# A feature-map attention followed by a maxout network, on one core: transposes by DMA, projections of q and k in banks of their own, stages by pair of heads

## The chip, the cores and the metric

The kernel runs on one core of a Trainium2 chip. A core has a matrix engine (TensorE, PE; loading its weights is shown as PEld), a vector engine (VectorE, DVE), a scalar engine (ScalarE, ACT), GpSimd (POOL) and Sync (SP), which here only issues DMAs; Sync, ACT and POOL each have a queue of DMAs, issued in program order. The metric is the time of one execution in microseconds; lower is better.

## The reference

For each of 8 x 8 heads, with 576 tokens of 64 elements, q and k are projected by `w_phi` to 128 features; the row's maximum of absolute values is subtracted, and both exponentials are kept. The result of the attention becomes the token matrix of a feed-forward network (FFN) with three up-projections, of which the elementwise maximum is kept.

```python
proj = x @ w_phi                                  # x is q or k: (8, 8, 576, 64) -> 128 features
proj = proj - max(abs(proj), axis=-1)
phi  = concat([exp(proj), exp(-proj)])            # 256 features
kv   = k_phi.T @ v ;  z = k_phi.sum(tokens)
x    = (q_phi @ kv) / (q_phi @ z + 1e-6)          # -> (4608, 512)
h    = maximum(maximum(x @ w1, x @ w2), x @ w3)   # 768 wide
out  = h @ w_out                                  # (4608, 512), float32
```

## The kernel before

The attention is cut into 16 **units** of 4 heads (half a batch entry). A unit has 18 blocks of 128 tokens: 4 for each head's first 512 tokens, and two that hold the 64 last tokens of two heads each. Its steps have one letter each, and an index for the piece:

- L loads q, k, v (Sync); C casts q and k to bf16 into `qk_bf`, side by side in 128 columns; T transposes the blocks on TensorE (L185) into PSUM, and DVE copies them to `qkT` (L186).
- G, for 4 blocks at a time, projects q and k in one matmul of 256 columns a block (L193, two banks, tag `g`); DVE reduces both to the maxima `m` (L196), ACT writes the two exponentials of k, `Ek` (L199).
- E scales v by exponentials of k's maxima (`em`), on POOL (L205 to L216). K multiplies `Ek` and the scaled v (L245) to `kv_sb`.
- Q and R put q's maxima into `mqp` and transpose them; V writes them by a DMA on ACT's queue as row 64 of `qkT` (L226). M projects q transposed, with a weight row of -1 that subtracts that row (L232), and ACT writes `Eq` (L234).
- N multiplies `Eq` and `kv_sb` (L258) and divides (`x_sb`); X transposes `x_sb` on TensorE (L272), and DVE copies it into `xT_main` and `xT_tail` (L273, L275).

When both units of a batch entry have passed X, a **chunk** of the FFN is queued: 18 "up" pieces of four matmuls of 512 columns (L287), evicted by ACT or DVE, and 4 "down" pieces of six (L302), evicted by ACT to `osb` and stored by Sync (L307). There are 8 chunks and one for all tails.

The order is written by hand: three lines of PROLOGUE, and PERIOD, which is run for u = 3 to 17; in `M4:1` the number behind the colon is the lag, so it is piece 4 of step M of unit u - 1. Each piece has a weight, and `run` puts FFN pieces between them until the line's budget (PRO_FFN, FFN_SHARE) is spread over it. Every engine works through its part of this order without reordering. PSUM is two pools: two buffers of two banks (G, K, N), four of one bank (all else).

Of the kernel before, what the change touches and what calls it, by code (L numbers as in the profile page):

```python
# [16 lines left out]
DF = 128  # L17
# [20 lines left out]
]  # L38
PERIOD = "X1:2 G0 L0:-2 G1 C0:-1 M4:1 M1:1 K0:1 G2 M0:1 C1:-1 G4 T0:-1 M2:1 G3 M3:1 N0:1 T1:-1 T2:-1 Q0 E0 N1:1 X0:1 R0 V0"
# [3 lines left out]
def kernel(  # L43
# [32 lines left out]
    raw = ctx.enter_context(tc.tile_pool(name="raw", bufs=2))  # L76
    vraw = ctx.enter_context(tc.tile_pool(name="vraw", bufs=3))
# [4 lines left out]
    psG = ctx.enter_context(tc.tile_pool(name="psG", bufs=2, space=bass.MemoryType.PSUM))  # L82
    psS = ctx.enter_context(tc.tile_pool(name="psS", bufs=4, space=bass.MemoryType.PSUM))

    class Unit:
        def __init__(un, u):
            un.u = u
            un.b = u // 2
            un.h0 = (u % 2) * HU
            un.ct0 = un.h0 // 2  # L90

        def load(un, what, engines=None, parts=1):
            for name, src in what:
                pool = vraw if name == "v_raw" else raw
                dst = pool.tile([P, UT, D], FP32, name=name, tag=name)
                setattr(un, name, dst)
                eng = (engines or {}).get(name, nc.sync)
                heads = src[un.b, un.h0:un.h0 + HU]
                n = HU // parts
                for i in range(parts):  # L100
                    h = slice(i * n, (i + 1) * n)
                    eng.dma_start(  # L102
                        dst[:, 4 * i * n:4 * (i + 1) * n, :].rearrange("p (h j) d -> p h (j d)", h=n),
                        heads[h, 0:SM, :].rearrange("h (p j) d -> p h (j d)", p=P))
                tails = heads[:, SM:S, :].rearrange("(pr ab) i d -> ab i pr d", ab=2)
                for ab in range(2):
                    eng.dma_start(dst[ab * D:(ab + 1) * D, MT:UT, :], tails[ab])  # L107

    first = Unit(0)
    first.load((("q_raw", q), ("k_raw", k)), {"k_raw": nc.scalar}, parts=2)  # L110
# [3 lines left out]
    wphi_f = const.tile([P, DF], FP32, name="wphi_f")  # L114
    nc.sync.dma_start(wphi_f[0:D, :], w_phi)
    nc.scalar.dma_start(wphi_f[D:2 * D, :], w_phi)
    first.load((("v_raw", v),))
# [26 lines left out]
    def load_w(half):  # L144
        n = slice(half * (DFF // 2), (half + 1) * (DFF // 2))
        for wi, w_ap in enumerate((moe_w1, moe_w2, moe_w3)):
            nc.gpsimd.dma_start(w_bf[wi][:, :, n], w_ap.rearrange("(ct p) n -> p ct n", p=P)[:, :, n])
# [4 lines left out]
    clock = [0]  # L152
    due = []

    def after(n, fn):
        due.append((clock[0] + n, fn))

    def piece(fn):
        fn()
        clock[0] += 1  # L160
        while True:
            now = [d for d in due if d[0] <= clock[0]]
            if not now:
                break
            due.remove(now[0])
            now[0][1]()
# [12 lines left out]
    def T(un, i):
        if i == 0:  # L180
            start_unit(un)
        t0, nb = ((0, 8), (8, 8), (16, 2))[i]
        tps = psS.tile([P, 8, P], BF16, name="tps", tag="s")
        for n in range(nb):
            nc.tensor.transpose(tps[:, n, :], un.qk_bf[:, t0 + n, :], ident)  # L185
        nc.vector.tensor_copy(un.qkT[:, t0 * P:(t0 + nb) * P],  # L186
                              tps[:, 0:nb, :].rearrange("p a c -> p (a c)"))

    def G(un, g):
        t0, n = GROUPS[g]  # L190
        psg = psG.tile([P, 4, 2, DF], FP32, name="psg", tag="g")
        for i in range(n):
            nc.tensor.matmul(psg[:, i, :, :].rearrange("p a f -> p (a f)"),  # L193
                             lhsT=un.qkT[:, (t0 + i) * P:(t0 + i + 1) * P],
                             rhs=w2.rearrange("p a f -> p (a f)"), start=True, stop=True)
        nc.vector.tensor_reduce(un.m[:, t0:t0 + n, :], psg[:, 0:n, :, :], AXX, ALU.max,  # L196
                                apply_absolute_value=True)
        for s in range(2):
            nc.scalar.activation(un.Ek[s][:, t0:t0 + n, :], psg[:, 0:n, 1, :], EXP,  # L199
                                 scale=1.0 - 2.0 * s)  # L200

    def E(un, i):
# [33 lines left out]
    def K(un, i):  # L236
        kvps = psG.tile([P, 2, 512], FP32, name="kvps", tag="g")
        W = D + 1
        for ab in range(2):
            for pr in range(2):  # L240
                for g in range(2):
                    o = (pr * 2 + g) * W
                    for c in range(5):
                        t = 8 * pr + 4 * ab + c if c < 4 else MT + pr
                        nc.tensor.matmul(kvps[:, ab, o:o + W], lhsT=un.Ek[g][:, t, :],  # L245
# [192 lines left out]
```

## Time and profile before

| | |
|---|---|
| median of 3 runs | 362.28 us (361.8 to 364.89) |
| the profiled execution | 361.97 us |
| its span, first to last instruction | 360.2 us |
| mean granted TensorE clock | 0.976 of 2.4 GHz |
| busy: PE, DVE, ACT, POOL | 314.7, 242.7, 217.6, 120.8 us |

The profile is of one execution. Spans of matmuls overlap, as they are pipelined: how far apart they start tells what one costs, and the chain of waits shows that for each run of them. "DMA share" is the mean busy share of the 16 DMA engines.

### The profile page before, as it was taken

The page shows a single profiled execution, that of the slowest core. Times are in us where ns is not written, and L with a number is a line of the kernel's source. Part 1 is how long each engine was busy: PE and PEld are TensorE (multiplying, and loading weights), DVE is VectorE, ACT ScalarE, POOL GpSimd, SP SyncE. Part 2 cuts the span into 40 slices and gives each one's busy share as a digit, 9 for nine tenths or more (in the row PEclk, how much of TensorE's full clock was granted, in tenths as well). Part 3 has the DMA queues.
Part 4 walks back from the last instruction along what each step waited for, and adds up shares of the span by engine and source line. Part 5 has one row for each costly group of instructions (what it writes and reads, how often), then busy time and mean ns, then how long its engine had stood idle before and what let it go on. Part 6 is the DMA issues. An engine that isn't in the chain of part 4 may idle for free.

```text
span 360.2 us, 7592 instructions
## 1 busy us (share of the span) xinstructions
PE 314.7 (87%) x2928; PEld 192.7 (54%) x2976; DVE 242.7 (67%) x403; ACT 217.6 (60%) x475; POOL 120.8 (34%) x164
## 2 busy tenths in 40 slices
PE   0656775899989997999899989997999999999994
PEld 0434653565646664666565656665666555544441
DVE  0674469688679866987698769876887775454350
ACT  2247375658676866767676867686859673522312
POOL 3342933434333434162516160707070505000000
PEclk9996689999999999999999999999999999999999
DMA  6898399512392229222832284217100200200205
GB/s 204 267 235 221 43 232 276 147 55 66 118 268 65 66 94 276 80 68 88 243 118 68 83 230 136 69 59 224 36 1 31 90 1 2 89 29 29 90 0 117
DMA packets 49028, 41.53 MB, mean 115 GB/s; under 512 B 15840, under 2 KB 44384, under 8 KB 48992
## 3 DMA queue, kind: packets, MB, share of 16 engines
q1 hardware_dynamic: 43696, 37.20, 34.1%
q0 software_dynamic: 3952, 3.15, 5.6%
q10 hardware_dynamic: 1344, 0.70, 0.7%
q8 instruction: 23, 0.38, 0.4%
q14 instruction: 13, 0.11, 0.1%
HBM read 34.67 MB, written 9.44 MB: 122 GB/s over the span
## 4 chain that ended last, share of the span: by engine, by line
PE 70%; issue 10%; DMA 10%; DVE 3%; POOL 2%; SPq 2%; ACT 1%; ACTq 0%; POOLq 0%; DVEq 0%
PE ups L287 32%; PE ops L302 13%; PE psg L193 7%; DMA qkT<-mT 5%; PE psn L258 5%; PE kvps L245 4%; PE tps L185 4%; PE psm L232 4%; DMA v_raw<-in_v_dram 3%; DVE m L196 2%; PE pxT L272 2%; DMA q_raw<-in_q_dram 1%; SPq L107 1%; POOL vtl L212 1%; SPq L102 1%
## 5 line engine op out<-in xcount | busy, mean ns | idle before, releaser
L287 PE MATMUL ups<-xT_main,w_bf 128*128 128x512 bf16 x540 | 141.7, 379 | 2.2 <-ACT t L291 0.3
L205 POOL TENSOR_TENSOR vab<-v_raw,em 128x2048 bf16<-128x2048 f32 x16 | 58.0, 3627 | 167.6 <-ACT em L204 131.5
L199 ACT ACTIVATE Ek<-psg 128x512 bf16<-128x512 f32 (+1 forms) x160 | 80.2, 555 | 44.3 <-DVE m L196 43.6
L196 DVE TENSOR_REDUCE m<-psg 128x8 f32<-128x1024 f32 (+1 forms) x80 | 87.9, 1115 | 27.7 <-PE psg L193 27.5
L287 PEld LDWEIGHTS <-w_bf 128*128 128x128 bf16 x648 | 60.2, 98 | 54.0 <-issue 1.2
L234 ACT ACTIVATE Eq<-psm 128x512 bf16<-128x512 f32 (+1 forms) x160 | 79.1, 573 | 8.4 <-PE psm L232 7.0
L291 ACT CAST t<-ups 128x512 bf16<-128x512 f32 x54 | 32.3, 598 | 50.6 <-PE ups L287 38.4
L193 PE MATMUL psg<-w,qkT 128*128 128x256 bf16 x288 | 45.5, 287 | 9.1 <-DVE m L196 4.3
L294 DVE TENSOR_TENSOR t<-t,ups 128x512 bf16<-128x512 bf16 x54 | 36.8, 681 | 23.1 <-PE ups L287 22.5
L302 PE MATMUL ops<-wout_bf,hT 128*128 128x512 bf16 x207 | 50.9, 379 | 0.5
L297 DVE TENSOR_TENSOR hT<-t,ups 128x512 bf16<-128x512 bf16 x54 | 37.1, 686 | 11.0 <-PE ups L287 7.6
L193 PEld LDWEIGHTS <-qkT 128*128 128x128 bf16 x288 | 28.6, 101 | 27.0 <-issue 5.9
L185 PE MATMUL tps<-ident,qk_bf 128*128 128x128 bf16 x288 | 25.9, 233 | 13.0 <-DVE qk_bf L352 11.5
L232 PE MATMUL psm<-qkT,wphi_m 128*128 128x512 bf16 (+1 forms) x78 | 26.2, 370 | 10.3 <-DMA qkT<-mT 8.2
L305 ACT COPY osb<-ops 128x512 f32<-128x512 f32 x36 | 21.3, 591 | 21.7 <-PE ops L302 21.2
L185 PEld LDWEIGHTS <-qk_bf 128*128 128x128 bf16 x288 | 21.2, 105 | 18.9 <-issue 12.2
L302 PEld LDWEIGHTS <-hT 128*128 128x128 bf16 x216 | 20.2, 98 | 19.9 <-DVE hT L297 0.4
L258 PE MATMUL psn<-kv_sb,Eq 128*128 128x65 bf16 x640 | 27.8, 198 | 3.2 <-ACT Eq L234 3.0
L258 PEld LDWEIGHTS <-Eq 128*128 128x128 bf16 x640 | 25.2, 100 | 9.0 <-ACT Eq L234 5.3
L186 DVE COPY qkT<-tps 128x1024 bf16<-128x1024 bf16 (+1 forms) x48 | 26.2, 552 | 3.9 <-PE tps L185 3.8
L264 DVE TENSOR_TENSOR x_sb<-psn,rden 128x640 bf16<-128x640 f32 x32 | 26.4, 825 | 1.1
L245 PEld LDWEIGHTS <-Ek 128*128 128x128 bf16 x640 | 23.6, 102 | 5.7 <-ACT Ek L199 3.8
(40 smaller groups left out, 234.9 us busy)
## 6 DMA issues: line engine op xcount, KB each, us to landing
v_raw<-in_v_dram SPq DMA_DIRECT2D x16, 512.0 KB, 4.3
out_dram<-osb SPq DMA_DIRECT2D x32, 256.0 KB, 2.3
q_raw<-in_q_dram SPq DMA_DIRECT2D x15, 512.0 KB, 4.8
k_raw<-in_k_dram SPq DMA_DIRECT2D x15, 512.0 KB, 5.0
w_bf<-in_moe_w_dram POOLq DMA_DIRECT2D x6, 384.0 KB, 8.6
q_raw<-in_q_dram SPq DMA_DIRECT2D x32, 32.0 KB, 4.6
v_raw<-in_v_dram SPq DMA_DIRECT2D x32, 32.0 KB, 4.3
out_dram<-osb SPq DMA_DIRECT2D x8, 128.0 KB, 2.3
```

The source lines that it names most:

```text
L185: nc.tensor.transpose(tps[:, n, :], un.qk_bf[:, t0 + n, :], ident)
L193: nc.tensor.matmul(psg[:, i, :, :].rearrange("p a f -> p (a f)"), lhsT=un.qkT[:, (t0 + i) * P:(t0 + i + 1) * P], rhs=w2.rearrange("p a f - ...
L196: nc.vector.tensor_reduce(un.m[:, t0:t0 + n, :], psg[:, 0:n, :, :], AXX, ALU.max, apply_absolute_value=True)
L199: nc.scalar.activation(un.Ek[s][:, t0:t0 + n, :], psg[:, 0:n, 1, :], EXP, scale=1.0 - 2.0 * s)
L205: nc.gpsimd.tensor_tensor(un.vab[:, :, :, 0:D], un.v_raw[:, 0:MT, :].unsqueeze(1).to_broadcast([P, 2, MT, D]), un.em[:, :, 0:MT].unsqueeze ...
L232: nc.tensor.matmul(psm[:, 0:n * P], lhsT=wphi_m, rhs=un.qkT[:, cols], start=True, stop=True)
L234: nc.scalar.activation(un.Eq[s][:, cols], psm[:, 0:n * P], EXP, scale=1.0 - 2.0 * s)
L245: nc.tensor.matmul(kvps[:, ab, o:o + W], lhsT=un.Ek[g][:, t, :], rhs=un.vab[:, g, t, :] if c < 4 else un.vtl[:, g, pr, ab, :], start=(c == ...
L258: nc.tensor.matmul(psn[:, ab, c * W:(c + 1) * W], lhsT=un.Eq[g][:, t0:t0 + P], rhs=un.kv_sb[:, ab, pr, g, :], start=(g == 0), stop=(g == 1))
L287: nc.tensor.matmul(ups, lhsT=w_bf[i][:, ct, j * P:(j + 1) * P], rhs=xT[:, ct, cols], start=(ct == 0), stop=(ct == CT - 1))
L297: nc.vector.tensor_tensor(hT[:, j, :], t_of.pop(j), ups, ALU.max)
L302: nc.tensor.matmul(ops_, lhsT=hT[:, j, tt * P:(tt + 1) * P], rhs=wout_bf[:, j, :], start=(j == 0), stop=(j == JT - 1))
```

## The change

- **Transposes by DMA.** Units 3 to 15 take `qkT` from two DMA transposes on Sync's queue (Y; 9 blocks each) in place of T; units 4 to 14 take `xT_main` and `xT_tail` from three (Z) in place of X. N writes the tails of those units to a tile of their own, `x_tail`.
- **G** writes k and q to a bank each (`psk`, `psq`), by a matmul of 128 columns for each block and each of the two, and DVE reduces them one by one; q's maxima go straight to `mqp` (Q is gone).
- **Maxima by matmul.** Units 0 and 1 use D in place of R, V and M: the same projection, and for each block a matmul of the broadcast maxima with a negative identity, added in PSUM.
- **By head pair.** A unit's blocks are ordered by pair of heads (9 and 9); loads, C (three pieces), E and K work on a pair or less. Unit 0 is loaded by single heads first. q, k have one raw buffer (two before), v two (three before).
- **PSUM** is eight single banks by kind: two for k, one pair for N, four for the rest. 14 matmuls on zeros run at the start (WARM).
- **Order and shares.** PROLOGUE's first line takes units 0 and 1 through all steps; A queues a chunk, with lag 2 in PERIOD. The loads of the FFN weights are cut into column blocks 1, 2 and 3 of 6. X's copy of the tails moves to ACT.

```diff
-FFN_SHARE = 10.0
-PRO_FFN = [2, 0, 0]
+PT = 9
+TBLOCKS = [(0, 4), (4, 12), (12, 18)]
+WBLOCKS = [(0, 1), (1, 3), (3, 6)]
+BANKS = {'k': 2, 'n': 1, 's': 4}
+BANK_OF = {'q': 's', 'v': 's', 'r': 's', 'm': 's', 'u': 's', 'd': 's'}
+WARM = 14
+FFN_SHARE = 8.9
+PRO_FFN = [4, 17, 8]
+XBAR = range(4, UNITS - 1)
+TBAR = range(3, UNITS - 0)
+YBLOCKS = [(0, 9), (9, 18)]
+YAT = {1: 0, 2: 1}
 PROLOGUE = [
...
+    "L0:-1 C0 C2 T0 C1 T1 T2 L1:-1 G0 G1 L1:-2 G2 D0 G3 C0:-1 C1:-1 D1 G4 C2:-1 E0 L0:-2 W1 T0:-1 E1 T1:-1 G0:-1 D3 T2:-1 W0 G1:-1 D2 D1:-1 D4 G2:-1 D0:-1 K0 E0:-1 G3:-1 N0 X0 G4:-1 K1 E1:-1 C1:-2 D2:-1 N1 D3:-1 K0:-1 C0:-2 K1:-1 X1 D4:-1 N0:-1 T0:-2 N1:-1 L1:-3 X0:-1 C2:-2 X1:-1 A0:-1 T1:-2 L0:-3 T2:-2 W2 C2:-3",
+    "L1:-2",
+    "C0:-1 G2 G4 C1:-1 T1:-1 G0 G1 G3 W3 T2:-1 E0 E1 R0 V0 L0:-2",
 ]
-PERIOD = "X1:2 G0 L0:-2 G1 C0:-1 M4:1 M1:1 K0:1 G2 M0:1 C1:-1 G4 T0:-1 M2:1 G3 M3:1 N0:1 T1:-1 T2:-1 Q0 E0 N1:1 X0:1 R0 V0"
+PERIOD = "G3 G0 C1:-1 K0:1 A0:2 C2:-1 M2:1 L1 G1 T2:-1 M0:1 M1:1 C0:-1 G2 T1:-1 M4:1 L0:-2 N0:1 E0 M3:1 K1:1 G4 E1 N1:1 X0:1 R0 V0 X1:1"
...
+    if WARM:
+        zeros = const.tile([P, SM], BF16, name="zeros")
+        nc.vector.memset(zeros, 0.0)
+        idle = bank([P, SM], FP32, "idle", "r")
+        for _ in range(WARM):
+            nc.tensor.matmul(idle, lhsT=zeros[:, 0:P], rhs=zeros, start=True, stop=True)
...
+    def Y(un, i):
+        if un.qkT is None:
+            start_unit(un)
+        t0, t1 = YBLOCKS[i]
+        nc.sync.dma_start_transpose(out=un.qkT[:, t0 * P:t1 * P].rearrange("p (t c) -> p t c", c=P),
+                                    in_=un.qk_bf[:, t0:t1, :].rearrange("p t c -> p (t c)"))
+
+    def Z(un, pr):
+        ct = un.ct0 + pr
+        nc.sync.dma_start_transpose(
+            out=xT_main[:, ct, un.b * SM:(un.b + 1) * SM].rearrange("p (c t) -> p c t", c=4),
+            in_=un.x_sb[pr][:, 0:4].rearrange("p c a d -> p (c a d)"))
+        if pr == 1:
+            nc.sync.dma_start_transpose(out=xT_tail[:, un.ct0:un.ct0 + 2, un.b * ST:(un.b + 1) * ST],
+                                        in_=un.x_tail.rearrange("p r d -> p (r d)"))
 
     def G(un, g):
         t0, n = GROUPS[g]
-        psg = psG.tile([P, 4, 2, DF], FP32, name="psg", tag="g")
-        for i in range(n):
-            nc.tensor.matmul(psg[:, i, :, :].rearrange("p a f -> p (a f)"),
-                             lhsT=un.qkT[:, (t0 + i) * P:(t0 + i + 1) * P],
-                             rhs=w2.rearrange("p a f -> p (a f)"), start=True, stop=True)
-        nc.vector.tensor_reduce(un.m[:, t0:t0 + n, :], psg[:, 0:n, :, :], AXX, ALU.max,
-                                apply_absolute_value=True)
...
+        psk = bank([P, 4, DF], FP32, "psk", "k")
+        psq = bank([P, 4, DF], FP32, "psq", "q")
+        for ab, ps in ((1, psk), (0, psq)):
+            for i in range(n):
+                nc.tensor.matmul(ps[:, i, :], lhsT=un.qkT[:, (t0 + i) * P:(t0 + i + 1) * P],
+                                 rhs=w2[:, ab, :], start=True, stop=True)
+        for ab, ps in ((1, psk), (0, psq)):
+            nc.vector.tensor_reduce((un.mqp, un.m)[ab][:, t0:t0 + n], ps[:, 0:n, :], AXX, ALU.max,
+                                    apply_absolute_value=True)
...
+    def D_(un, g):
+        t0, n = GROUPS[g]
+        cols = slice(t0 * P, (t0 + n) * P)
+        psm = bank([P, 4 * P], FP32, "psm", "m")
+        nc.tensor.matmul(psm[:, 0:n * P], lhsT=w2[:, 0, :], rhs=un.qkT[:, cols], start=True, stop=False)
+        for i in range(n):
+            nc.tensor.matmul(psm[:, i * P:(i + 1) * P],
+                             lhsT=un.mqp[:, t0 + i:t0 + i + 1].to_broadcast([P, P]),
+                             rhs=negident, start=False, stop=(i == n - 1))
+        for s in range(2):
+            nc.scalar.activation(un.Eq[s][:, cols], psm[:, 0:n * P], EXP, scale=1.0 - 2.0 * s)
...
+    def A(un, i):
+        if un.u % 2 == 1:
+            main_chunk(un.b)
+        if un.u == UNITS - 1:
+            tail_chunk()
```

## Rows read from the trace of the kernel before

**Rows 1.** The page's head and its first part.

```profile
span 360.2 us, 7592 instructions
...
PE 314.7 (87%) x2928; PEld 192.7 (54%) x2976; DVE 242.7 (67%) x403; ACT 217.6 (60%) x475; POOL 120.8 (34%) x164
```

**Rows 2.** Windows: span, length, busy us and instructions per engine, PE clock, DMA share, GB/s.

```profile
20.00:30.00 10.00, 5.09 (x35) 3.90 (x36) 8.18 (x11) 4.82 (x11) 5.25 (x6) 0.95 1.22 248
30.00:40.00 10.00, 7.12 (x76) 4.81 (x77) 2.69 (x7) 7.07 (x18) 4.48 (x4) 0.50 0.40 108
...
13.84:53.40 39.56, 26.56 (x260) 19.52 (x262) 23.19 (x37) 22.77 (x52) 21.02 (x27) 0.78 0.91 195
171.45:208.06 36.61, 34.87 (x355) 22.00 (x360) 28.82 (x49) 26.22 (x58) 14.39 (x19) 1.00 0.41 127
...
302.30:360.20 57.90, 52.88 (x295) 25.19 (x300) 22.41 (x36) 17.80 (x31) 0.00 (x0) 1.00 0.18 55
```

**Rows 3.** The chain of waits in order of time: start us, length us, what.

```profile
9.71 1.03 PE tps L185 x8
...
14.67 0.85 PE tps L185 x8
...
208.06 3.57 DMA qkT<-mT
...
212.18 0.86 PE ups L287 x4
213.04 1.26 PE kvps L245 x40
...
217.77 0.45 PE tps L185 x8
...
219.29 0.44 PE psg L193 x4
...
220.81 0.62 PE psn L258 x20
...
225.21 0.28 PE pxT L272 x5
...
235.77 1.29 PE ops L302 x6
```

**Rows 4.** The timeline of PE, 0 to 60 us: the first matmul of the FFN.

```profile
59.67 0.38 PE L287 MATMUL ups<-xT_main,w_bf 128*128 128x512 bf16 x1
```

**Rows 5.** Waits of PE: us in total, times, longest.

```profile
PE psm L232 <- DMA qkT<-mT: 8.2, 6, 2.0
```

**Rows 6.** Groups by line and shape, DVE: count, busy us, mean ns of one, idle before.

```profile
L196 DVE TENSOR_REDUCE m<-psg 128x8 f32<-128x1024 f32 x64 | 77.0, 1222 | 26.3 <-PE psg L193 26.1
...
L186 DVE COPY qkT<-tps 128x1024 bf16<-128x1024 bf16 x32 | 21.9, 684 | 2.5 <-PE tps L185 2.5
...
L273 DVE COPY xT_main<-pxT 128x512 bf16<-128x512 bf16 x32 | 13.4, 419 | 4.8 <-PE pxT L272 4.8
...
L196 DVE TENSOR_REDUCE m<-psg 128x4 f32<-128x512 f32 x16 | 11.0, 685 | 1.4 <-PE psg L193 1.4
```

**Rows 7.** The timeline of Sync's queue, 200 to 240 us.

```profile
208.78 1.26 SPq L107 DMA_DIRECT2D q_raw<-in_q_dram  x2
210.14 0.54 SPq L102 DMA_DIRECT2D k_raw<-in_k_dram  x1
...
237.71 0.36 SPq L307 DMA_DIRECT2D out_dram<-osb  x1
```

**Rows 8.** The timeline of ACT, 204 to 222 us: its queue issuing a DMA.

```profile
208.06 0.73 ACTq L226 DMA_DIRECT2D qkT<-mT  x1
```

**Rows 9.** DMA queues (packets, MB, share of 16 engines) and issues (KB, us to landing).

```profile
q1 hardware_dynamic: 43696, 37.20, 34.1%
...
out_dram<-osb SPq DMA_DIRECT2D x32, 256.0 KB, 2.3
...
wout_bf<-in_moe_w_out_dram POOLq DMA_DIRECT2D x1, 768.0 KB, 11.8
```

More of the change, by code (lines that the diff above doesn't have):

```diff
@@ L90, in __init__, with view, alloc @@
             un.ct0 = un.h0 // 2
-        def load(un, what, engines=None, parts=1):
-            for name, src in what:
+            un.qk_bf = un.qkT = None
+        def view(un, dst):
+            return dst.rearrange("p (r t) d -> p r t d", r=2)
+        def alloc(un, name):
+            if un.u == 0:
+                dst = const.tile([P, UT, D], FP32, name=name + "0")
+            else:
                 pool = vraw if name == "v_raw" else raw
                 dst = pool.tile([P, UT, D], FP32, name=name, tag=name)
[L96 to L107, printed above, removed]
@@ L109, with load_main @@
-    first = Unit(0)
-    first.load((("q_raw", q), ("k_raw", k)), {"k_raw": nc.scalar}, parts=2)
+            setattr(un, name, dst)
+            return un.view(dst)
+        def load_main(un, eng, dst, src, heads):
+            n = heads.stop - heads.start
+            pr, a0 = heads.start // 2, heads.start % 2
+            eng.dma_start(dst[:, pr, 4 * a0:4 * (a0 + n), :].rearrange("p (ab j) d -> p ab (j d)", ab=n),
+                          src[un.b, un.h0 + heads.start:un.h0 + heads.stop, 0:SM, :]
+                          .rearrange("ab (p j) d -> p ab (j d)", p=P))
@@ new lines, in load_tails, with load @@
+        def load_tails(un, eng, dst, src):
+            tails = src[un.b, un.h0:un.h0 + HU, SM:S, :].rearrange("(pr ab) i d -> ab i pr d", ab=2)
+            for ab in range(2):
+                eng.dma_start(dst[ab * D:(ab + 1) * D, :, 8, :], tails[ab])
+        def load(un, what):
+            for name, src in what:
+                dst = un.alloc(name)
+                for pr in range(2):
+                    un.load_main(nc.sync, dst, src, slice(2 * pr, 2 * pr + 2))
+                un.load_tails(nc.sync, dst, src)
@@ L112 @@
+    for ab in range(2):
+        nc.gpsimd.dma_start(wphi_f[ab * D:(ab + 1) * D, :], w_phi)
+    first.load((("v_raw", v),))
     ident = const.tile([P, P], BF16, name="ident")
     make_identity(nc, ident)
[L114 to L117, printed above, removed]
+    negident = const.tile([P, P], BF16, name="negident")
+    nc.gpsimd.tensor_single_scalar(negident, ident, -1.0, ALU.mult)
@@ L142, with load_w @@
     xT_tail = const.tile([P, CT, B * ST], BF16, name="xT_tail")
[L144 to L147, printed above, removed]
+    def load_w(n0, n1):
+        for w, w_ap in zip(w_bf, (moe_w1, moe_w2, moe_w3)):
+            nc.gpsimd.dma_start(w[:, :, n0:n1], w_ap.rearrange("(ct p) n -> p ct n", p=P)[:, :, n0:n1])
@@ L149, in load_wout, with copy @@
     def load_wout():
         nc.gpsimd.dma_start(wout_bf, moe_w_out.rearrange("(ct p) n -> p ct n", p=P))
[L152 to L166, printed above, removed]
+    def copy(eng, dst, src):
+        if eng is nc.scalar:
+            eng.copy(dst, src)
+        else:
+            eng.tensor_copy(dst, src)
@@ L238, in K @@
+    def K(un, pr):
+        kvps = bank([P, 2, 2 * (D + 1)], FP32, "kvps", "v")
         W = D + 1
         for ab in range(2):
[L240 to L245, printed above, removed]
-                                         rhs=un.vab[:, g, t, :] if c < 4 else un.vtl[:, g, pr, ab, :],
-                                         start=(c == 0), stop=(c == 4))
@@ L248, in K @@
-        un.kv_sb = mpool.tile([P, 2, 2, 2, W], BF16, name="kv_sb", tag="kv_sb")
-        nc.vector.tensor_copy(un.kv_sb.rearrange("p a r g d -> p a (r g d)"), kvps[:, :, 0:4 * W])
+            for g in range(2):
+                for c in range(5):
+                    t = PT * pr + (4 * ab + c if c < 4 else 8)
+                    nc.tensor.matmul(kvps[:, ab, g * W:(g + 1) * W], lhsT=un.Ek[g][:, t, :],
+                                     rhs=un.vab[:, g, t, :] if c < 4 else un.vtl[:, g, pr, ab, :],
+                                     start=(c == 0), stop=(c == 4))
@@ L333, in run @@
     def run(pieces, budget):
-        total = sum(w for w, _ in pieces)
+        total = sum(w for w, _ in pieces) or 1.0
         have = done = 0.0
         for w, fn in pieces:
-            piece(fn)
+            fn()
             have += w
@@ L396, in tokens @@
             name, i, lag = word[0], int(word[1]), int(word[3:]) if ":" in word else 0
+            if name == "X" and u - lag in XBAR:
+                name = "Z"
+            if name == "T" and u - lag in TBAR:
+                if i not in YAT:
+                    continue
+                name, i = "Y", YAT[i]
             got += stage(name, i, u - lag)
```

151 lines of the change are left out of this document (84 added, 67 removed), and 3 rows, old and new, of the table PROLOGUE.

## The prediction

> **What bounds the kernel now.** I read the page's totals first [rows 1]: TensorE is busy 314.7 of 360.2 us, the others 67% at most. The windows then show three stages [rows 2]. From 60 us on, two units take 36.61 us, 34.87 of them busy on PE: TensorE sets the pace, with DVE at 28.8 and ACT at 26.2. From 302 us only the feed-forward network (FFN) is left, and PE is busy 52.9 of 57.9 us. Up to 53 us it is not the bound: it is busy 26.6 of 39.6 us, and slowly, for the granted clock is 0.50 (1.2 GHz) from 30 to 40 us, and eight transposes took 0.85 us at 14.67 against 0.45 at 217.77 [rows 3]. The first matmul stands at 9.71 us and the first FFN matmul at 59.67 [rows 3, 4].
>
> The chain in order of time prices a piece once TensorE runs at speed [rows 3]: 0.056 us for a transpose (0.45/8; 0.28/5 for x), 0.11 for a matmul of 256 columns, 0.215 for one of 512, 0.0315 for one of K, 0.031 for one of N, 0.86 for an "up" of four, 1.29 for a "down" of six. A unit is then 18 x 0.109 (G) + 18 x 0.056 (T) + 0.97 (M) + 1.26 (K) + 1.25 (N) + 0.56 (X) + 0.06 (R) + half a chunk of FFN, 10.36, in all 17.4 us. The measured 18.3 leaves 0.9, most of it one wait per pair for the row of maxima (qkT<-mT, 3.57 us on the chain; psm waits 8.2 us for it in all) [rows 3, 5].
>
> The same count rebuilds the whole run: 60 us of prologue, 13 periods of 18.3 (238), 14.3 for the 16th, 41.7 for the last two chunks, 5 at the end (57.9 less 52.9): 359, against a span of 360.2. The profiled execution took 361.97 us, 1.8 more than its span; the median of the three runs is 362.28.
>
> **Transposes leave TensorE.** Units 3 to 15 lose 18 transposes, units 4 to 14 ten more: 1.0 and 0.56 us of PE a unit, all of it on the path, as PE is dense there: 13.1 + 6.2 = 19 us. DVE loses their evictions, of which the large ones are 2 x 0.684 + 2 x 0.42 a unit [rows 6].
>
> **What replaces them on the queues.** A unit gets two transposes for q and k (295 KB each), two for x (131 KB) and one for the tails (33 KB). No row shows one. Sync's queue spends 0.54 us on a main load, 0.63 on a tail (1.26 for two), 0.36 on an output [rows 7], and ACT's 0.73 on the SBUF-to-SBUF row of maxima [rows 8]. Six mains and six tails (the loads are now split by head pair) and two outputs make 7.7 us a unit; five transposes at 0.36 to 0.73 make 1.8 to 3.7 more, and I take 0.73, an SBUF-to-SBUF issue being nearest: 11.4 of a period of 15.3. They reach the path only if the queue's sum passes the period.
>
> Landing is bounded by 2.3 us (an output) and 11.8 (the casting weight load) [rows 9]. The first transpose of the next unit is issued in the middle of a period and the second two pieces later; the first G needs them when the next period begins, 5 to 8 us later, so I cost them nothing; if one took the 11.8, G would wait some 4 us each period. On the DMA engines, q1's 43,696 packets took 34.1% of 16 x 360.2 us: 45 ns each, 7.7 us a unit [rows 9]. Counted in 256-byte rows the transposes are 3,456 packets a unit, 9.7 us more at that price; the packets of now average 851 bytes, so I take half, 4.9: 12.6 of 15.3. The Trainium skill speaks against the change: "VectorE: DVE Perf Modes", section "The three transpose paths", gives 1309 ns for a 128x128 bf16 block by DMA against 390 on TensorE, and advises TensorE where PSUM will do. By that page of the Trainium skill, block after block, a unit's 27 blocks would be an estimated 35 us. The Trainium skill's "Advanced Engine Details and Errata", section "X-Bar Transpose (TRN2)", makes such DMAs as fast as ordinary ones at 350 to 400 GB/s, an estimated 2.5 us for the unit's 0.88 MB. No run here shows either; TensorE's own block costs 0.056 us on the dense chain.
>
> The queue also gains waits. q and k have one raw buffer now, so the load for the next unit but one waits for POOL's casts of the next one; behind it on Sync's queue stand the x transposes, which wait for x_sb, and the outputs, whose four buffers ACT fills. The casts come in thirds and E in halves by head pair, which takes POOL from 7.2 us a unit to 9 at the most likely, as only its small pieces double: of 15.3, no bound [rows 2]. The order puts the casts ahead of that load by two pieces and more, so I cost this at nothing; if the cover fails, the queue stands still for a cast, and the fall of the second rival begins.
>
> **G in two banks.** 36 matmuls of 128 columns for 18 of 256. The nearest row is the transpose, which also loads weights each time: 36 x 0.056 = 2.0 against 1.96, nothing; at the price of a 256-column one each it would be +2.0 a unit, the upper bound. DVE reduces eight halves at 0.685 for four at 1.222, +0.6 a unit [rows 6], paid by the evictions: 14.4 falls to about 12. ACT stays near 13.1, plus a second pair of small exponentials and the 0.73 issue: about 14, under a 15.3 us period but close.
>
> **The period.** PE work per unit in periods 5 to 15: G 2.0, K 1.26, N 1.25, M 0.97, R 0.06, and FFN 8.9 (a piece's weight in the code is about its us, and the budgets place 98 in these 11 periods): 14.4. M2 now stands behind G3, G0, K0 and three FFN pieces, some 4 us, against the row's 3.57 us, so that wait nearly goes. What is late next is ACT, whose exponentials free the banks that G and the FFN share. I take 0.9 again, between 0.1 (nothing waits) and 2.6: 15.3, between 14.5 and 17.
>
> **The prologue.** The first two units are finished before anything else, without the V round trip: D subtracts the maxima by 36 further matmuls (2 us at 0.056, 4 at half clock, beside ACT). Loads by head let the first transpose start some 3.5 us earlier; 14 idle matmuls run where PE waits for data until 9.71 us now; they cost nothing if they end by then (14 x 0.43 at half clock is 6 us). The copies of x tails by ACT in the five units that keep X are ten of 64 columns, in ACT's sum below. ACT was busy 22.8 us from 13.8 to 53.4 for about this work [rows 2]; it will have 24, and at 80% it takes 30. From 8 us that is 38, and 41 with the last N and X. Then 4.35 us of FFN, and unit 2's G with 7.8 of FFN (the budget 17 of the second line buys nothing, its only piece weighing 0): period 3 starts near 55.5 instead of 60, with 12.2 us of FFN done. Bounds: 50 and 66, the upper one if weights come late: some 13 MB must have landed by then, 53 us at the 248 GB/s of 20 to 30 us [rows 2].
>
> **What it gives back.** The second chunk is queued only in period 5 (A0 with lag 2), so period 3 uses up the first and period 4 has none: ACT-bound, 12 us with 6 of PE work.
>
> **The sum.** 55.5 + 15.5 (period 3) + 12 + 11 x 15.3 + 13.8 (period 16) + 60 (18.2 left of the seventh chunk, and 41.7 of the last two, dense as now) + 5 = 330.1, and 1.8 around the span: 331.9. I forecast 332 us.
>
> **Rivals.** (1) The prologue and ACT keep the gain: PE stays at 1.2 GHz between short bursts, weights come late, period 3 starts at 62, and ACT at 14 us a period costs 0.8 more in each: 332 + 6.5 + 9 = 347. For it: the half clock of 30 to 40 us; against: FFN now comes earlier and is dense. (2) Slower: Sync's queue becomes the bound. Loads, outputs, transposes stand in one order, and a transpose holds all behind it. 7.7 + 5t passes 15.3 at t = 1.5 us a transpose and loses the whole gain at about t = 1.95, where the period is 17.4; at 2.2 it is 18.7, and 332 + 11 x 3.4 + 6.7 (period 4) = 376. Against it: no issue on Sync's queue shown takes over 0.63; for it: none of those writes by the block. (3) The DMA engines bind: at 45 ns a packet they need 17.4 us a unit: 332 + 11 x 2.1 + 5.4 (period 4) = 360, no change. The 1309 ns block of the Trainium skill's page "VectorE: DVE Perf Modes" would end here too, at an estimated 550 us and more. (4) All waits vanish (11 x 0.8 less) and the prologue ends 4 us sooner: 319. (5) That the change doesn't do what it says: the first units alone keep their transposes on PE, so 13 of 16 must vanish; I give it nothing.
>
> **How the numbers follow.** Forecast 0.58 (own range 325 to 342), (1) 0.22, (2) 0.08, (3) 0.06, (4) 0.06. Faster by over 1%, about what this kernel's runs can tell from no change, has 0.86; within it 0.06; slower 0.08. The range 319 to 357 leaves out (2) and (3), 0.14, and the far ends of the rest.
>
> **What would show it.** Right: no tps in the dense stretch; a period of 15 to 15.6 us with PE busy 94%; no psm wait on qkT<-mT; an FFN matmul by 46 us; an idle period near 70 us; over 55 us of pure FFN at the end. Wrong: psg waiting for DMA on qkT, transposes of 1.5 us and more on Sync's queue, a DMA share near 1, or Ek and Eq as PE's releasers all along.

## The result and the profile after

The changed kernel takes 352.9 us against 362.2, a ratio of 0.9715 (95% interval 0.9644 to 0.9786): faster by 2.9%, a third of the forecast 8.4%. The profiled execution took 352.68 us. Here and below, executions over 1.5% above the fastest of their kernel are in the medians, but not in the ratios nor in the columns that a table takes from profiles. I read the profile in the order of [rows 1, 2]: totals, then the dense stretch, here from the transpose of unit 4's maxima to that of unit 15's (periods 5 to 15).

The page's head, its lines of PE, PEclk and DMA in 40 slices, and its first DMA queue:

```profile
span 350.9 us, 7981 instructions
...
PE 306.9 (87%) x2968; PEld 180.6 (51%) x2968; DVE 217.4 (62%) x412; ACT 216.4 (62%) x518; POOL 147.8 (42%) x296
...
PE   6665895696699999899999799989989999999994
...
PEclk9999699699899999999999899999999999999999
DMA  7898977748957678675969657959771210301205
...
q1 hardware_dynamic: 89152, 48.36, 53.6%
```

The dense stretch (columns as in [rows 2]):

```profile
93.17:272.20 179.03, 166.63 (x1802) 102.49 (x1800) 132.41 (x259) 135.16 (x333) 93.78 (x188) 0.98 0.71 179
```

Eleven periods take 16.28 us each, where [rows 2] show 18.3 and I forecast 15.3; DVE (12.0 us a period) and ACT (12.3) have room. Between those transposes the periods are far from even: 15.2 to 15.8 us in seven, 16.5, 17.1 and 19.3 in three, and 17.8 in the first. The first FFN matmul stands at 41.02 us (forecast 41), where [rows 4] had 59.67. Two things stand out.

**The start of period 3.** The chain in order of time:

```profile
52.69 1.19 POOL qk_bf L201 x2
...
53.90 1.57 SPq L224
...
55.52 8.55 DMA qkT<-qk_bf
...
64.11 0.60 PE psk L245 x4
```

TensorE stands still for 7.0 us, until the second transpose of unit 3's q and k lands, 8.55 us after its issue; the median of all 26 is 3.3. At 53.8 us POOL had issued the load of the output weights, which took 8.6 us to land. Afterwards the clock is at its lower level: 0.66 granted from 60 to 70 us, 0.50 from 64.1 to 66.7, where an up takes twice its 0.86.

**The held row of maxima.** ACT's timeline, then the chain, in the longest period:

```profile
190.27 0.25 ACT L279 COPY mT<-pmT 18x128 bf16<-18x128 bf16 x1
193.66 0.73 ACTq L283 DMA_DIRECT2D qkT<-mT  x1
194.44 2.06 ACT L251 ACTIVATE Ek<-psk 128x512 bf16<-128x512 f32 x4 [3.91 <-DVE kv_sb L317]
```

```profile
188.55 1.97 DMA q_raw<-in_q_dram
190.52 3.13 issue
193.66 2.51 DMA qkT<-mT
...
196.21 0.39 PE psm L289
```

The maxima are ready at 190.52, but V leaves ACT's queue at 193.66, and the exponentials queued behind it wait with it. (kv_sb, which the row names as the releaser, was written from 193.91 to 194.32 us; V's own issue, ahead of them on the queue, ended at 194.39.) The chain puts V behind a load of q. In the trace the DMAs of Sync's and ACT's queues take eight semaphores in turn, so V also waits for the DMA eight places before it, here the load of q issued at 188.55: ACT's queue waits on that semaphore, the last of the load's 16 pieces lands at 193.59, and V leaves at 193.66. In [rows 8] V left as soon as it could, 0.03 us after the copy of the maxima. TensorE waits 2.4 us for this V and then works at its lower clock, 0.57 granted from 196 to 200 us, where an up again takes twice its 0.86 (197.46 to 199.16): the period is long by the wait and by the clock behind it.

TensorE's waits from 93 to 272 us, which answer to [rows 5]:

```profile
PE psm L289 <- DMA qkT<-mT: 5.3, 3, 2.4
PE ups L361 <- ACT Eq L291: 3.7, 9, 0.6
PE psk L245 <- DMA qkT<-qk_bf: 0.9, 1, 0.9
```

Sync's queue across the same period, which answers to [rows 7]:

```profile
188.55 1.28 SPq L129 DMA_DIRECT2D q_raw<-in_q_dram  x2
189.87 1.11 SPq L122 DMA_DIRECT2D k_raw<-in_k_dram  x2
191.02 1.71 SPq L129 DMA_DIRECT2D k_raw<-in_k_dram  x2
192.83 2.58 SPq L229 DMA_TRANSPOSE xT_main<-x_sb  x2
195.50 1.19 SPq L233 DMA_TRANSPOSE xT_tail<-x_tail  x1
196.75 1.09 SPq L122 DMA_DIRECT2D v_raw<-in_v_dram  x2
197.88 1.28 SPq L129 DMA_DIRECT2D v_raw<-in_v_dram  x2
199.26 1.34 SPq L224 DMA_TRANSPOSE qkT<-qk_bf  x1
203.78 0.38 SPq L381 DMA_DIRECT2D out_dram<-osb  x1
204.26 1.31 SPq L224 DMA_TRANSPOSE qkT<-qk_bf  x1
205.62 1.09 SPq L122 DMA_DIRECT2D q_raw<-in_q_dram  x2
```

It issues without a pause from 188.55 to 200.6, then stands behind an output whose buffer ACT has not filled, and the next unit's transpose and loads stand behind that output. The transposes by line (ns: least, median, most):

```profile
L224 SPq DMA_TRANSPOSE qkT<-qk_bf x26: 1242/1324/3895, 53.9 to 253.9; - x26
...
L229 SPq DMA_TRANSPOSE xT_main<-x_sb x22: 1195/1239/2265, 111.8 to 272.5; - x22
...
L233 SPq DMA_TRANSPOSE xT_tail<-x_tail x11: 1185/1185/1287, 114.6 to 273.8; - x11
```

Five a unit are 2 x 1.32 + 2 x 1.24 + 1.19 = 6.3 us, not 3.7.

### The profile page after: what moved, and what is told of

It is laid out like the page before. It is cut to its first block, busy times and chain, and to the rows that moved or that the text cites. A ratio compares the mean times of both kernels' runs of the same rounds, so it can differ in the third digit from the quotient of the medians.

```text
span 350.9 us, 7981 instructions
## 1 busy us (share of the span) xinstructions
PE 306.9 (87%) x2968; PEld 180.6 (51%) x2968; DVE 217.4 (62%) x412; ACT 216.4 (62%) x518; POOL 147.8 (42%) x296
## 3 DMA queue, kind: packets, MB, share of 16 engines
q1 hardware_dynamic: 89152, 48.36, 53.6%
## 4 chain that ended last, share of the span: by engine, by line
PE 48%; ACT 22%; DMA 13%; SPq 6%; DVE 5%; issue 3%; POOL 3%; ACTq 0%; POOLq 0%; DVEq 0%
PE ups L361 28%; PE ops L376 8%; ACT Ek L251 8%; ACT Eq L291 8%; DMA q_raw<-in_q_dram 5%; DMA qkT<-qk_bf 4%; PE psn L326 4%; SPq L224 3%; DMA qkT<-mT 2%; PE kvps L312 2%; ACT Eq L303 2%; PE psk L245 2%; ACT t L365 2%; PE psq L245 2%; PE psm L289 1%
## 5 line engine op out<-in xcount | busy, mean ns | idle before, releaser
L251 ACT ACTIVATE Ek<-psk 128x512 bf16<-128x512 f32 (+1 forms) x160 | 82.1, 587 | 44.0 <-DVE m L248 22.1
L262 POOL TENSOR_TENSOR vab<-v_raw,em 128x1024 bf16<-128x1024 f32 x32 | 61.1, 1909 | 89.2 <-ACT em L260 67.6
L291 ACT ACTIVATE Eq<-psm 128x512 bf16<-128x512 f32 (+1 forms) x140 | 71.6, 617 | 3.9 <-PE psm L289 3.7
L248 DVE TENSOR_REDUCE m<-psk 128x4 f32<-128x512 f32 (+1 forms) x80 | 50.5, 632 | 30.2 <-PE psk L245 29.9
L245 PEld LDWEIGHTS <-qkT 128*128 128x128 bf16 x576 | 39.3, 101 | 25.6 <-DMA qkT<-qk_bf 8.9
L248 DVE TENSOR_REDUCE mqp<-psq 128x4 bf16<-128x512 f32 (+1 forms) x80 | 50.1, 627 | 0.0
L245 PE MATMUL psk<-w,qkT 128*128 128x128 bf16 x288 | 30.2, 224 | 10.8 <-DMA qkT<-qk_bf 8.1
L289 PE MATMUL psm<-qkT,wphi_m 128*128 128x512 bf16 (+1 forms) x70 | 24.7, 362 | 8.2 <-DMA qkT<-mT 7.5
L376 PEld LDWEIGHTS <-hT 128*128 128x128 bf16 x216 | 20.0, 98 | 22.5 <-issue 1.7
L245 PE MATMUL psq<-w,qkT 128*128 128x128 bf16 x288 | 30.1, 224 | 0.1
L201 POOL CAST qk_bf<-k_raw 128x512 bf16<-128x512 f32 (+2 forms) x43 | 21.3, 518 | 18.0 <-DMA k_raw<-in_k_dram 18.0
L312 PE MATMUL kvps<-vab,Ek 128*128 128x65 bf16 x512 | 25.3, 195 | 2.7 <-POOL vab L266 2.3
```

Of the source, the lines that this page charges most:

```text
L245: nc.tensor.matmul(ps[:, i, :], lhsT=un.qkT[:, (t0 + i) * P:(t0 + i + 1) * P], rhs=w2[:, ab, :], start=True, stop=True)
L248: nc.vector.tensor_reduce((un.mqp, un.m)[ab][:, t0:t0 + n], ps[:, 0:n, :], AXX, ALU.max, apply_absolute_value=True)
L251: nc.scalar.activation(un.Ek[s][:, t0:t0 + n, :], psk[:, 0:n, :], EXP, scale=1.0 - 2.0 * s)
L262: eng.tensor_tensor(un.vab[:, :, t0:tt, 0:D], un.v_raw[:, t0:tt, :].unsqueeze(1).to_broadcast([P, 2, 8, D]), un.em[:, :, t0:tt].unsqueeze( ...
L291: nc.scalar.activation(un.Eq[s][:, cols], psm[:, 0:n * P], EXP, scale=1.0 - 2.0 * s)
L312: nc.tensor.matmul(kvps[:, ab, g * W:(g + 1) * W], lhsT=un.Ek[g][:, t, :], rhs=un.vab[:, g, t, :] if c < 4 else un.vtl[:, g, pr, ab, :], s ...
```

## The experiments

Theory 1: V is held by the semaphore that it shares with a load, and the supply of weights delays period 3. Theory 2: the transposes' traffic slows every transfer. Theory 3: ACT is the bound at its margin. Theory 4 came after run 5: Sync's queue is too full. Medians in us; ratios to the kernel before, on the same chip, since the kernel before took 362.2 to 365.2 us on the chips used (0.8%). To compare two runs, divide their ratios. P3 is period 3, and "mean" that of periods 5 to 15, from the one profiled execution of each run; runs 5 and 16 have none, and run 16's ratio rests on two executions. The expectations call run 5 "run 4" once, and run 9 "run 5".

| run | us | ratio (95%) | P3 | mean |
|---|---|---|---|---|
| the change | 352.9 | 0.9715 (0.9644 to 0.9786) | 23.5 | 16.28 |
| 1 V on POOL, R moved | 355.6 | 0.9766 (0.9717 to 0.9815) | 21.7 | 16.55 |
| 2 output weights later | 352.8 | 0.9699 (0.9651 to 0.9746) | 25.3 | 16.22 |
| 3 x on TensorE | 360.1 | 0.9888 (0.9839 to 0.9936) | 22.5 | 16.77 |
| 4 q, k on TensorE | 373.1 | 1.0254 (1.0206 to 1.0302) | 22.1 | 17.64 |
| 5 tail loads after V | 361.6 | 0.9941 (0.9906 to 0.9977) | | |
| 6 no output weights | 347.2 | 0.9559 (0.9522 to 0.9597) | 17.9 | 16.31 |
| 7 FFN from P3 to P4 | 350.7 | 0.9656 (0.9607 to 0.9706) | 21.9 | 16.24 |
| 8 runs 2, 5 and 7 | 358.7 | 0.9863 (0.9809 to 0.9916) | 14.3 | 16.90 |
| 9 v loads on POOL | 348.6 | 0.9554 (0.9496 to 0.9611) | 22.7 | 15.58 |
| 10 one transpose for q, k | 354.6 | 0.9736 (0.9684 to 0.9787) | 23.2 | 16.40 |
| 11 v's tails thrice | 407.9 | 1.1206 (1.115 to 1.1263) | 24.7 | 20.85 |
| 12 runs 2, 7, 9 and 10 | 353.5 | 0.9713 (0.9662 to 0.9765) | 15.9 | 16.44 |
| 13 V on POOL, R in place | 352.5 | 0.9674 (0.9608 to 0.9741) | 22.9 | 16.34 |
| 14 runs 9 and 13 | 350.2 | 0.9621 (0.9572 to 0.9671) | 22.8 | 15.99 |
| 15 runs 2, 7 and 9 | 346.8 | 0.9509 (0.946 to 0.9559) | 15.6 | 16.02 |
| 16 runs 2, 7, 9 and 13 | 349.3 | 0.9511 (0.9436 to 0.9585) | | |

**Run 1**

```diff
-        nc.scalar.dma_start(un.qkT[D:D + 1, :]...
+        nc.gpsimd.dma_start(un.qkT[D:D + 1, :]...
-PERIOD = "... K1:1 G4 E1 N1:1 X0:1 R0 V0 X1:1"
+PERIOD = "... K1:1 G4 R0 V0 E1 N1:1 X0:1 X1:1"   # and E0 R0 V0 E1 in the prologue
```

> The row of maxima (V) is issued from POOL's queue instead of ACT's, after the transpose of the maxima; all else stands. Theory 1 (in the changed kernel V stands at the head of ACT's queue up to 3.1 us after mT is there, because its semaphore is one of eight that all DMAs of Sync's and ACT's queues share, and the DMA eight places before it is a load issued just before; the exponentials behind it stand still with it): the issue comes within 0.3 us of mT in every period, the psm<-mT waits fall under 1 us, the eleven periods 5 to 15 go from 16.2 towards 15.4 us each, and the time falls by 6 to 9 us, to 344 to 347. Theory 2 (the transposes' traffic slows every transfer, V's own among them): V still lands late, the periods stay at 16.2, the time within 1.5 us of 352.9. Theory 3 (ACT is the bound at its margin): the periods stay at 16.2 and ACT's idle time moves elsewhere, time within 2 us. POOL's own issue of a DMA costs it about 1 us of a queue that has room for it.

A miss that settles nothing: the waits for qkT<-mT fell away, but the earlier R made TensorE wait 0.74 to 1.46 us a period for DVE's maxima (11.3 us over periods 5 to 15). Run 13 repeats it without that.

**Run 2**

```diff
-    "... G0 G1 G3 W3 T2:-1 E0 E1 R0 V0 L0:-2",
+    "... G0 G1 G3 T2:-1 E0 E1 R0 V0 L0:-2 W3",
```

> The 1.57 MB load of the output weights (wout) is issued at the end of the prologue's third line, after the loads of the next unit, and not ahead of unit 2's exponentials; all else stands. Theory 1 (period 3 begins 7 us late because unit 3's q and k transposes, issued at 55.5, land only at 64.1 beside this load): the landing falls from 8.6 us to about 3, the wait psk<-qkT at the start of period 3 from 7.0 us to under 2, and the time falls by 4 to 7 us, to 346 to 349. Theory 2 (the transposes are late because the casts before them wait for k to be loaded; the load of wout is an innocent neighbour): the landing stays over 6 us or the wait stays over 5, and the time within 2 us of 352.9. The first down product may wait up to 2 us for the weights.

Half right. The wait for the transposes fell from 7.0 to 0.7 us, so the load of the weights was what they were late beside; the time stayed, since the weights themselves then came late. TensorE's waits from 54 to 94 us:

```profile
PE ops L376 <- DMA wout_bf<-in_moe_w_out_dram: 7.1, 1, 7.1
...
PE psk L245 <- DMA qkT<-qk_bf: 0.7, 1, 0.7
```

**Runs 3 and 4**

```diff
-XBAR = range(4, UNITS - 1)
+XBAR = range(0)                     # run 3
-TBAR = range(3, UNITS - 0)
+TBAR = range(0)                     # run 4, with T0:-1 ahead of T1:-1
```

> The x transposes alone go back to TensorE with their evictions on VectorE and ScalarE (no Z on Sync's queue); q and k keep the DMA transposes. By the forecast's own terms the x transposes are worth 6.2 us of TensorE over the dense periods: with TensorE as the bound the time would rise by 4 to 6, to 357 to 359. If instead waits on transfers are what the periods are made of (theory 1 or 2), taking 11 Z pairs off the queue and a quarter of the added packets off the DMA engines pays part of it back, and the time stays within 2 us of 352.9; if it falls below 351, the Z transposes cost more than the TensorE work that they remove.

> The q and k transposes alone go back to TensorE with their evictions on VectorE (no Y on Sync's queue); x keeps the DMA transposes. By the forecast's own terms they are worth 13.1 us of TensorE over 13 units. If TensorE is the bound and nothing else moves: 352.9 + 13 = 366. If the losses come from the late first transposes of unit 3 and the held V (theory 1), the start of period 3 gets its 7 us back and V waits for less, so the time is 352.9 + 13 - 7 - some of the 9, that is 350 to 359. If the transposes' traffic slows every load (theory 2), as little as 348.

x on TensorE costs 1.8% (0.9888 over 0.9715), 6 us: the forecast's 6.2. q and k cost 5.5%, 19 us, more than the 13.1 of TensorE's work that they put back: TensorE now waits for the casts where Sync's queue had waited for it. Its largest waits, 95 to 272 us:

```profile
PE tps L217 <- ACT qk_bf L199: 10.9, 10, 1.4
...
PE tps L217 <- POOL qk_bf L201: 2.5, 5, 0.7
```

So neither group of DMA transposes is itself a loss here.

**Run 5**

```diff
-... M4:1 L0:-2 N0:1 ... X0:1 R0 V0 X1:1
+... M4:1 L3:-2 N0:1 ... X0:1 R0 V0 L2:-2 X1:1   # L3: mains, L2: tails of q and k
```

> In the periods only, the four small tail loads of q and k are issued after the row of maxima (V) instead of before it; V stays on ACT's queue and the order of all compute stands. The DMA eight places before V, whose semaphore V shares, is then no load of the same period in most periods. This is the clean form of the first run, which moved the transpose of the maxima too and so made TensorE wait 0.74 to 1.46 us a period for DVE's maxima. Theory 1 (the held V is what makes 16.2 of 15.4): V follows mT within 0.3 us in most periods, the psm<-mT waits of 1.3 to 2.4 us go, the long periods (16.5 to 19.3) become 15.2 to 15.7, and the time falls by 5 to 9 us, to 344 to 348. Theory 2 (the transposes' traffic) and theory 3 (ACT at its margin): the long periods stay, within 1.5 us of 352.9.

The sign is wrong: slower by 2.3% than the change. The chain shows why theory 1's remedy failed, and started theory 4 (it is of an execution of 364.1 us, so it is read for its order and not for its lengths):

```profile
138.59 1.74 SPq L224
...
140.44 1.28 SPq L224
...
142.57 0.47 SPq L122
...
143.09 4.74 DMA k_raw<-in_k_dram
...
147.93 2.10 DMA qkT<-mT
```

V now waits for a load of k, and ahead of that stands Sync's queue issuing back to back: whichever load V shares its semaphore with is a late one.

**Run 6**

```diff
-        nc.gpsimd.dma_start(wout_bf, moe_w_out...)
+        nc.gpsimd.memset(wout_bf, 0.01)
```

> The load of the output weights is left out and replaced by a constant written by POOL, so the output products use a constant. Run 2 moved this load and swapped a 7.0 us wait for the q and k transposes of unit 3 for a 7.15 us wait for the weights. Theory 1 (what the DMA engines must carry by 72 us is the limit there): with 1.57 MB less both waits go, period 3 falls from 23.5 to 16 to 18 us and the time by 5 to 8, to 345 to 348. Rival (the transposes are late by themselves, since the casts wait for k): the wait psk<-qkT stays over 5 us and the time within 2 us of 352.9.

As theory 1 said: period 3 falls by 5.6 us and the time by 1.6%. With run 2, the wait is for the weights or for what lands beside them, and moving the load moves the wait. It is not shown that the DMA engines are the limit up to 72 us: in the changed kernel their share is 1.12 from 40 to 50 us, but 0.04 from 50 to 54, just before the load is issued. An earlier issue was not tried.

**Runs 7 and 8**

```diff
-        run(tokens(PERIOD, u), FFN_SHARE)
+        run(tokens(PERIOD, u), {3: 3.5}.get(u, FFN_SHARE))
```

> Period 3 takes 3.5 us of the feed-forward network instead of 8.9, so that about 5 us of it (the four products with the output weights) come in period 4, which has none now. Theory 1: period 3 goes from 23.5 to 18 to 20, period 4 from 12.8 to 14 to 15, and period 5 (17.8) loses its stretch at half clock: the time falls by 3 to 5 us, to 348 to 350. Theory 3 (periods 3 and 4 are bound by ACT whatever TensorE does): within 1.5 us of 352.9.

> The three together: tail loads after the maxima, the output weights loaded after the next unit's loads, and 5 us of the feed-forward network moved from period 3 to period 4, so that the weights are wanted some 7 us later. Theory 1: the waits for unit 3's transposes and for the weights both vanish, periods 5 to 15 average 15.4: 352.9 less 7 less 8 less 3 to 4, 334 to 339, close to the forecast. If the causes overlap (a stall hidden behind another), 340 to 346. Theories 2 and 3: no more than 4 us.

Run 7 can't be told from the change. Run 8 shortens period 3 to 14.3 us, pays 5.6 back in period 4 (18.4), and loses the rest in periods 5 to 15 (16.90 us), where run 5's edit acts.

**Run 9**

```diff
-                    un.load_main(nc.sync, dst, src, ...)
+                    un.load_main(eng, dst, src, ...)        # tails likewise
-        un.load(... (("v_raw", v),))
+        un.load(... (("v_raw", v),), nc.gpsimd if i and un.u > 3 else nc.sync)
```

> From unit 4 on the four loads of v are issued from POOL's queue instead of Sync's; all else stands. Run 4 of theory 1 (tails after the maxima) went the wrong way, 361.6, and its trace shows Sync's queue issuing without a pause; in the changed kernel the median issues of a unit add up to 13.7 us (six mains 0.5, six tails 0.61, 1.8 outputs 0.39, two transposes of q and k 1.32, two of x 1.24, one of the tails 1.19), with the gaps some 14.6 of a period of 15.4. Theory 4 (Sync's queue is as full as TensorE: any wait in it makes the loads late, V is held by such a load, casts wait): 2.2 us less on the queue bring the periods to 15.3 to 15.6, the waits psm<-mT and qk_bf<-k_raw go, and the time falls by 5 to 9 us, to 344 to 348. Theory 2 (traffic) and theory 3 (ACT): within 1.5 us of 352.9, as the bytes and ACT's work are the same.

Theory 4 holds: 1.7% faster than the change with the same bytes, more DMA time (share 0.77) and the same work on ACT, against theories 2 and 3. The dense stretch, and TensorE's waits from 93 to 272 us:

```profile
93.93:265.30 171.37, 163.51 (x1802) 100.53 (x1800) 131.93 (x259) 135.39 (x333) 123.01 (x232) 1.00 0.77 187
```

```profile
PE ups L361 <- ACT Eq L291: 3.3, 7, 0.6
PE psm L289 <- DMA qkT<-mT: 1.0, 3, 0.5
```

15.58 us a period, 15.40 without the first: the forecast's 15.3. The profiled execution took 345.8 us, the fastest of the four and 2.8 under their median, so 15.58 is at the low end; the ratios give 5.9 us, some 0.5 a period.

That V takes its semaphore behind other DMAs is not what changed: it stands behind a load of q in eight of the eleven periods, in the changed kernel as in run 9. But in run 9 those loads are issued 2.8 to 4.7 us before the maxima are ready, in the three held periods of the changed kernel only 1.1 to 2.5. The loads of v also go by POOL's own DMA queue now, which no run separates from their leaving Sync's.

**Runs 10 and 11**

```diff
-YBLOCKS = [(0, 9), (9, 18)]
+YBLOCKS = [(0, 18)]                 # run 10, at T1's place
-                un.load_tails(nc.sync, dst, src)
+                for _ in range(3 if name == "v_raw" and un.u > 3 else 1):
+                    un.load_tails(nc.sync, dst, src)      # run 11
```

> One transpose of 18 blocks for q and k instead of two of 9, issued where the later of the two stood; all else stands. The issues of 295, 131 and 33 KB take 1.32, 1.24 and 1.19 us, so nearly all of the cost goes with the DMA and not with its bytes. Theory 4: the queue saves about 1.2 us a unit, at the price of a landing of 5 us or so in place of 3.3; the time falls by 2 to 6 us, to 347 to 351. Rival (the issue cost goes with the blocks, or the late landing makes the first G of each period wait 1 to 2 us): 353 to 365.

> From unit 4 on the two tail loads of v are issued three times instead of once, the same data to the same place: four more issues of 0.61 us on Sync's queue a unit, with 3% more bytes. Theory 4 (Sync's queue is full): the queue needs 17 of a 15.4 us period, so the periods grow by 1 to 2.4 us and the time by 10 to 28 us, to 363 to 381. Theories 1, 2 and 3 (a shared semaphore in the order as it stands, traffic, ACT): within 3 us of 352.9, as far as the held V is not shifted by the new count of DMAs.

Run 10 misses, as its rival said: the one transpose takes the queue 2.87 us, as long as the two, and lands 4.7 us after its issue, and TensorE waits for it 6.4 us from 93 to 273 us. Run 11 grows by 15% over the change, well past the 381 us expected. It is more than the four issues, because each repeat also waits on the queue for the one before to land (32.7 us of Sync's waits); what it shows is where a longer queue goes. TensorE's waits:

```profile
PE psk L246 <- DMA qkT<-qk_bf: 33.7, 9, 6.4
```

**Run 12**, the edits of runs 2, 7, 9 and 10 together.

> Loads of v on POOL's queue, one transpose for q and k, the output weights loaded after the next unit's loads, and 5 us of the feed-forward network moved from period 3 to period 4. Theory 4 with the supply at the start of period 3: the periods at 15.3 (less 9), the start of period 3 without its 7 us wait, and 2 to 3 us from the moved products: 334 to 340, near the forecast. If the late landing of the one large transpose shows, 340 to 348.

A miss: it has run 10's late landings in it (6.1 us to landing, and TensorE waits for them 8.2 us from 92 to 273 us), and is no better than the change.

**Runs 13 to 16**

```diff
-        nc.scalar.dma_start(un.qkT[D:D + 1, :]...
+        nc.gpsimd.dma_start(un.qkT[D:D + 1, :]...
-PERIOD = "... G4 E1 N1:1 X0:1 R0 V0 X1:1"
+PERIOD = "... G4 N1:1 X0:1 R0 V0 E1 X1:1"     # run 13 (E0 R0 V0 E1 in the prologue); 14 to 16 join edits above
```

> V is issued from POOL's queue, where no load stands on its semaphore; the transpose of the maxima (R) keeps its place after N, and only the second half of E (exponentials of the maxima and POOL's products) moves behind V. Sync's queue carries what it carried. Theory 1 (the shared semaphore holds V, and that is the loss): no wait pmT<-mqp as in run 1, none of psm<-mT over 0.5 us, periods 5 to 15 at 15.3 to 15.6, the time 4 to 8 us below 352.9: 345 to 349. Theory 4 (the full queue, whatever V waits for): the waits turn up at psk<-qkT instead, the periods stay over 16 and the time within 2 us of 352.9.

Theory 4's outcome: V's waits shrink, and the wait for late transposes takes their place, 16.34 us a period. POOL, on which V now stands, is not what makes them late: from 153 us on each transpose of q and k is issued 1.8 to 5.1 us after the last of the casts that it reads, right behind loads of v, an output or the transpose before it on Sync's queue. TensorE's waits, 93 to 272 us:

```profile
PE psk L245 <- DMA qkT<-qk_bf: 5.3, 5, 2.6
PE psm L289 <- DMA qkT<-mT: 3.5, 4, 1.2
```

> As the run before, and the loads of v on POOL's queue too (run 5: 348.6). If theories 1 and 4 are one loss seen from two ends, the time is that of the better of the two alone, within 1.5 us. If they are separate, 2 to 4 us below it. POOL's queue then carries five more DMAs a unit beside 8.5 us of work; if it becomes late in its turn, over 350.

> Run 5 (loads of v on POOL's queue, 348.6) with the output weights loaded after the next unit's loads and 5 us of the feed-forward network moved from period 3 to 4. If the loss at the start of period 3 is separate: 3 to 5 us below run 5, 343 to 346. If the supply at that place only moves on (as when the weights were moved alone): within 1.5 us of run 5.

> All of the three runs ahead together: V and the loads of v on POOL's queue, the second half of E behind V, the output weights later, 5 us of the network moved. If all losses add: 339 to 344; if they are shared, the best of the three runs ahead within 1.5 us.

Freeing V adds nothing to freeing the queue (14 against 9), which fits one loss, seen from two ends, but does not show it: 350.2 us is also what was expected if POOL's queue becomes late in its turn, and it does. Sync's transposes of q and k wait for POOL's casts 13.8 us from 93 to 272 us, in run 9 6.8. Run 15 is the best version, 4.9% under the kernel before (run 16 the same within its interval). Its periods 3 and 4 take 32.7 us for the change's 36.3, but one later period of 19.2 us, with V held again behind a load, gives most of that back (there POOL's four issues of v, 2.6 us, stand ahead of a cast, and Sync's transposes and loads behind that cast); against run 9 the intervals overlap, so how much of the start's loss is recovered stays open.

## Why the prediction was right or wrong

The direction, the range and the mechanism on TensorE were right, the size was not: two terms failed, Sync's queue in periods 5 to 15 and the weights' supply in period 3. The trace's own span exceeds the forecast's 330.1 by 20.8 us, and the pieces are: start of period 3 +1.4 (56.9 for 55.5), period 3 +8.0 (23.5 for 15.5), period 4 +0.8 (12.8 for 12), periods 5 to 15 +10.7 (11 x 16.28 = 179.0 for 168.3), the rest -0.1 (78.7 for 78.8).

- **What replaces them on the queues: the step that failed.** A transpose was priced at 0.73 us of Sync's queue, nearest to V's issue; it took 1.19 to 1.32. 7.7 + 6.3 makes 14.0 of 15.3, not 11.4. Worse was the rule that the issues "reach the path only if the queue's sum passes the period", with 1.5 us as the second rival's point. The queue waits in order, for x_sb, for osb and for casts, and what stands behind is late as soon as little room is left to make up for it. The waits that the queue gains, of which the prediction says "I cost this at nothing", are part of this. At 14.0 it cost some 0.5 to 0.7 us a period, 6 us of the 10.7 by run 9's ratio and 8 by its profiled execution. The second rival had the right place and the wrong point from which it decides.
- **V.** "That wait nearly goes" failed in the three held periods. The chain names V's shared semaphore, but run 13 shows that it is only the first to hand on the queue's lateness: without that semaphore the transposes of q and k, late on the same queue, make TensorE wait. Most of what run 9 gains lies in these three periods (16.5, 19.3 and 17.1 us, then 14.8, 15.7 and 15.8).
- **The rest of periods 5 to 15.** The first of them is long in both, but not for one reason. In the changed kernel (17.8 us) TensorE comes from the idle period 4 at its lower clock, 0.50 granted from 94.2 to 97.4 us (four matmuls of 128 columns take 0.63 us at 95.16 and 0.39 at 100.55). In run 9 (17.3 us) the clock is 1.00 throughout, and TensorE waits 2.1 us in it, where the changed kernel waits 1.4.
- **The period's work.** TensorE's 14.4 us and 0.9 of waits were right in their sum, for run 9's periods after the first take 15.40, though partly by luck: it is busy 14.9 us a period there (163.51 over 11), which leaves 0.7. G in two banks at +-0 was right (four blocks of one bank take 0.22 us, 0.056 each). DVE's 12 was right, ACT's 14 was 12.3 of busy time.
- **The prologue and weights: the second step that failed.** The start of period 3 was near its forecast, but the period, costed as a dense one at 15.5 us, took 23.5. The weights' supply, put at nothing unless it moved that start, was the cause of the 7.0 us wait (runs 2 and 6). The clock fell in that wait, and TensorE worked at its lower level for 2.6 us behind it. The first rival named the weights; ACT was not the cause, and the clock only followed. Without the load period 3 still takes 17.9 us (run 6), and what makes up the rest is open.
- **Landing and DMA engines.** 3.3 us of landing lie in cover in the steady periods, as said; added packets cost about 23 ns (q1: 53.6% of 16 x 350.9 less 34.1% of 16 x 360.2, over 45,456), 5.0 us for each of 13 units, for 4.9.
- **End and transposes.** The last two chunks and the end were right to 0.1 us; x's transposes are worth 6 us, as costed.
- **The price by the block.** By the Trainium skill, "VectorE: DVE Perf Modes", section "The three transpose paths", q's and k's nine blocks would be an estimated 11.8 us a DMA; the trace has 1.32 us of issue and 3.3 to landing, so the measurement decides against that price for these SBUF-to-SBUF transposes.

## What to carry to other kernels

A queue in program order can be late well before its issues fill the period (here at 14.0 us of 15.3): add up its issues at measured prices, and ask of each wait in it what stands behind. If one wait is taken away and another of the same size comes up, look for what both depend on, and relieve that (here four loads on another queue). A change that brings work forward must also have its data by then: sum the bytes due at each point, not at the end of the stage only.

## What the runs showed of the hardware

- A DMA transpose costs its queue 1.19 us for 33 KB, 1.24 for 131 and 1.32 for 295, but 2.87 for 590 (medians, the changed kernel and run 10): nearly flat, then not.
- A DMA on one queue can be held by the landing of a load on another, where they take the same semaphore: 3.1 us at 190.5 in the changed kernel, the load landing at 193.59 and the DMA leaving at 193.66.
